# A recurrence and gated-MLP kernel: second products of tiles 5 to 7 in float16 parts, chunk ends copied by ScalarE, and GpSimd's work moved to VectorE in a new order

## The chip, the cores and the metric

The kernel runs on one core of a Trainium2 chip. The metric is device time in microseconds, the median of several executions. One further execution is profiled; its trace gives every duration below.

## The reference

Two computations follow each other. The first is a gated linear recurrence over 768 steps for 4 batches of 8 heads of 48 dimensions; the second is an MLP on the 3072 tokens that come out, with 384 inputs, 2048 hidden units and 384 outputs.

```python
f = 1.0 / (1.0 + np.exp(-f_logit))
for t in range(S):
    state = f[:, :, t, :, None] * state + einsum('bhd,bhe->bhde', k[:, :, t], v[:, :, t])
    y[:, :, t] = einsum('bhd,bhde->bhe', q[:, :, t], state)
x = y.transpose(0, 2, 1, 3).reshape(B * S, H * D)
h = x @ w_in
g = h * np.clip(h + 3.0, 0.0, 6.0) / 6.0
out = g @ w_out
```

## The kernel before

**Work and stages.** Time is cut into 6 chunks of 128 steps; a unit is one chunk of one batch, so there are 24 units, numbered 0 to 23 (unit i is chunk i // 4). Four units of one chunk make a group of 512 tokens for the MLP, so there are 6 groups. The 2048 hidden units are 16 tiles of 128; step `mm1.20` is the first product of tile 20 % 16 = 4 in group 20 // 16 = 1.

**A unit.** `gate` (ScalarE) takes the sigmoid of the gates. `back` (VectorE, line 428) is a scan from the right over a chunk: it gives the suffix products of the gates, in a buffer `suffix` of which there are three. `kmul` (line 441) multiplies k by them. Column 0 of the suffix buffer is then the product over the whole chunk, the chunk end. `turn` (step `rend`, lines 444 and 445) limits it from below into `ends`, and writes the reciprocal into `rend`. `fwd` (line 448) scans from the left, starting at `rend`, and overwrites the same suffix buffer; `qmul` (line 454) multiplies q by the result. `decay` multiplies the batch's state by `ends`. TensorE transposes k (`tk`, line 516), multiplies k and v (`kv`, 537), k and q (`att`, 497), q and the state (`qs`, 571), and, after `mask` (VectorE, line 504), the masked square and v (`av`, 587).

**The MLP.** Weights come as 64-bit floats and are turned by `z`, `cy`, `mid`, `dif`, `top`, `high` and `low` (or `lowi` and `lowo`, the halves of `low` for the first and the second product, line 320) into one 32-bit form (`wide`) and two float16 parts (`weight`). A first product of a tile takes nine float16 matmuls: three of the four pairs of parts times three blocks of the 384 inputs. In group 0, tiles 0 to 4 are computed in two halves of 256 tokens (`mm1a`, `mm1b`, line 828, with second products in float32, line 846). Tiles 5 to 7 have a whole first product (`mm1`, line 664), then `relu` and `g`, and a second product `mm2x` in float32 (line 720). From tile 8 on, `gh` (ScalarE, line 683) and `gl` (VectorE, line 693) split the activation into two float16 parts, and `mm2` (line 709) takes nine float16 matmuls:

```python
def mm2(g, f, ms=range(KT)):
    for i in range(3):
        a, b = P3[-i]
        for m in ms:
            nc.tensor.matmul(g["o"][m], wout[:, f, a, m * 128:(m + 1) * 128], g[f]["gg"][:, b], ...)

def mm2_whole(g, f):
    for m in range(KT):
        nc.tensor.matmul(g["o"][m], wide_out(f, m), g[f]["t"], ...)
```

Groups 2 to 5 compute first products by `p1` to `p8` (line 772), with sums of weight blocks.

**What sets the order.** The list `ORDER` names some 1,560 steps. Each engine, and the queue of SyncE that starts the loads, executes its share of the list strictly in that order. Step `warm.n` is a matmul on zeros of n blocks of 128 columns (line 1071), whose result nobody reads. `ON_POOL` lists the elementwise steps that run on GpSimd; all others of their kind run on VectorE.

Of the kernel before, what the change touches and what calls it, by code (L numbers as in the profile page):

```python
# [58 lines left out]
z.0 mid.0 loadq.2 gate.3 back.3 ld.1 carry0.1 warm.1 qs.1.0 dif.0 kmul.2 top.0 fwd.2 xl.0 carry1.1 loadq.3 av.1 hole.0
tk.2.4 rend.3 xh.1 xs.1 xl.1 z.1 qmul.2 warm.5 att.2.2 kmul.3 cy.1 mid.1 fwd.3 ktok.2 loadv.2 high.0 warm.4 kv.2.1  # L60
carry0.2 tk.3.4 ktok.3 mask.2 load.4 gate.4 qs.2.0 hole.1 av.2 xh.2 carry1.2 lowi.0 mm1a.0.4 relua.0 dif.1 qmul.3
top.1 high.1 ga.0 loadv.3 xs.2 att.3.2 mask.3 kv.3.1 ld.2 carry0.3 carry1.3 lowi.1 xl.2 loadq.4 warm.1 qs.3.2 av.3
xh.3 mm1a.1.4 cy.2 xs.3 xl.3 relua.1 z.2 back.4 kmul.4 rend.4 fwd.4 ga.1 decay.4 mm2a.0 qmul.4 load.5 gate.5 tk.4.1
mm2a.1 ktok.4 loadv.4 ld.3 cy.3 z.3 hole.2 mid.2 dif.2 top.2 att.4.2 kv.4.3 hole.3 mm1b.0.0 high.2 back.5 mid.3
relub.0 loadq.5 mm1b.1.1 relub.1 lowi.2 gb.0 dif.3 kmul.5 rend.5 gb.1 mm1a.2.4 mm1b.2.0 top.3 mm2b.0 mm2b.1 fwd.5
tk.5.1 relua.2 relub.2 gb.2 qmul.5 ld.4 z.4 cy.4 mid.4 mm2b.2 high.3 ktok.5 lowi.3 ga.2 mm1b.3.0 load.6 gate.6 loadq.6
dif.4 back.6 top.4 load.7 mm1a.3.4 ld.5 relub.3 mm2a.2 relua.3 ga.3 high.4 gb.3 cy.5 z.5 mask.4 mm2a.3 lowi.4 mm1a.4.1
relua.4 rend.6 ld.6 mm1b.4.4 relub.4 loadv.6 gate.7 loadq.7 mm2b.3 carry0.4 kmul.6 fwd.6 mid.5 ga.4 dif.5 z.6 qmul.6
top.5 cy.6 tk.6.1 ktok.6 mm2a.4 back.7 ld.7 decay.5 high.5 qs.4.2 decay.6 att.5.0 gb.4 av.4 kv.6.1 carry1.4 lowi.5
mm1.5.4 mask.5 mm2b.4 carry0.6 xh.4 z.7 xl.4 mid.6 dif.6 kmul.7 carry1.6 loadv.5 kv.5.3 ld.8 relu.5 g.5 mm2x.5 cy.7  # L70
top.6 high.6 cy.8 rend.7 tk.7.0 mid.7 dif.7 load.8 lowi.6 carry0.5 top.7 mm1.6.4 ktok.7 qs.5.2 fwd.7 qmul.7 high.7
loadv.7 relu.6 g.6 z.8 decay.7 att.6.0 ld.9 lowi.7 gate.8 av.5 cy.9 z.9 mask.6 mm1.7.4 relu.7 mid.8 dif.8 top.8 mid.9
carry1.5 dif.9 high.8 low.8 mm2x.6 mm1.8.0 g.7 loadq.8 ld.10 top.9 xh.5 cy.10 relu.8 high.9 back.8 rend.8 mm2x.7 ld.11
xl.5 g.8 att.7.2 z.10 cy.11 qs.6.0 kv.7.3 mid.10 load.10 loadv.8 av.6 dif.10 low.9 top.10 z.11 mid.11 gh.8 mm1.9.4
ld.12 ld.14 xh.6 xl.6 gl.8 mm2.8 dif.11 high.10 low.10 relu.9 g.9 cy.12 mm1.10.1 top.11 mask.7 kmul.8 carry0.7 gh.9
gl.9 hole.4 relu.10 high.11 mm2.9 carry1.7 g.10 low.11 z.12 mid.12 ld.13 dif.12 top.12 cy.13 gh.10 gl.10 tk.8.1 ktok.8
mm1.11.0 z.13 high.12 qs.7.2 mm2.10 av.7 loadq.9 ld.15 kv.8.3 decay.8 relu.11 mid.13 dif.13 low.12 loadv.9 mm1.12.1
g.11 gh.11 xh.7 top.13 carry0.8 high.13 xl.7 hole.7 gl.11 relu.12 z.14 z.15 low.13 fwd.8 qmul.8 mm2.11 g.12 gh.12
mm1.13.4 relu.13 g.13 cy.14 gh.13 gl.13 gl.12 mm2.12 cy.15 qs.8.2 mid.14 dif.14 att.8.0 mask.8 lowo.0 top.14 high.14
hole.6 hole.5 mm1.16.4 load.9 mid.15 mm1.17.1 relu.16 carry1.8 relu.17 dif.15 ws1.0 g.16 mm1.20.0 g.17 loadq.11 low.14  # L80
gate.10 xtop.0 gate.9 mm1.18.1 load.11 top.15 relu.18 loadq.10 back.9 high.15 gh.16 av.8 back.10 mm1.14.4 g.18 mm2.13
lowo.4 gh.17 relu.14 low.15 g.14 gh.14 mm1.15.1 mm1.19.4 lowo.6 gh.18 kmul.9 gl.18 rend.9 relu.15 g.15 lowo.3 gh.15
gl.14 gl.15 tk.9.1 lowo.5 lowo.1 mm2.14 fwd.9 mm2.15 gl.16 ktok.9 gl.17 outs.2 loadv.11 lowo.7 outv.1 outs.0 mm1.23.1
mm2.16 gate.11 lowo.2 ws2.0 relu.19 od.0 ws3.0 mm2.17 rend.10 xh.8 g.19 back.11 od.2 kmul.10 relu.20 decay.9 relu.23
kmul.11 hole.8 fwd.10 rend.11 od.1 load.13 qmul.10 xsum.0.2 g.20 g.23 mm1.21.4 relu.21 load.12 xleast.0 tk.10.3 ws4.0
qmul.9 decay.10 ktok.10 mm2.18 gh.19 g.21 mm1.25.3 gh.20 mm1.24.2 gh.21 loadv.10 gate.12 wtop.4 gl.19 relu.24 att.9.1
relu.25 kv.9.0 gl.20 fwd.11 g.25 carry0.9 loadv.12 g.24 wsh.0 load.14 qmul.11 mm1.22.4 gate.13 relu.22 back.12 gh.24
mm2.19 tk.11.3 gl.21 ws1.1 mask.9 gh.23 carry1.9 ktok.11 mm2.20 g.22 qs.9.0 att.11.3 gate.14 loadq.12 gh.25 gl.25 av.9
# [1150 lines left out]
```

## Time and profile before

| | us |
|---|---|
| median of 3 executions (lowest, highest) | 459.32 (459.2, 459.85) |
| the profiled execution: its time | 459.1 |
| the profiled execution: its span | 457.4 |
| TensorE busy in the span | 449.4 (98%) |
| VectorE busy | 359.3 (79%) |
| ScalarE busy | 231.2 (51%) |
| GpSimd busy | 19.0 (4%) |

The span runs from the first to the last instruction of the execution; 1.7 us of its time lie around it. Busy time is the union of an engine's records, and neighbouring records overlap a little, so the distance from one start to the next is a better price of an instruction in a full queue than its duration.

### The profile page before, as it was taken

To read this page: it belongs to the slowest core of one execution; us is meant where nothing else is said; L and a number is where in the kernel's file an instruction comes from. 1 tells how busy PE (TensorE), PEld (TensorE's weight loads), DVE (VectorE), ACT (ScalarE), POOL (GpSimd) and SP (SyncE) were. 2 spreads that over 40 slices of the span, in tenths; PEclk is the share of its full clock that TensorE was granted. 3 is DMA by queue.
4 is the path that set the end of the run, shared out by engine and by line. 5 is a ranking of instruction groups with operands and counts; after the bars stand their busy time and mean duration, and the time that the engine had idled before them with its cause. 6 is when DMAs were issued, how large, how long until landed. Compare 5 with 4: busy or idle time off the path is not lost.

```text
span 457.4 us, 12555 instructions
## 1 busy us (share of the span) xinstructions
PE 449.4 (98%) x5445; PEld 292.8 (64%) x5449; DVE 359.3 (79%) x643; ACT 231.2 (51%) x389; POOL 19.0 (4%) x31
## 2 busy tenths in 40 slices
...
GB/s 283 223 251 385 225 189 251 203 155 16 52 125 99 158 52 59 108 3 120 89 1 85 78 142 18 21 143 2 1 10 1 5 29 2 1 115 2 1 0 73
DMA packets 25531, 43.18 MB, mean 94 GB/s; under 512 B 2560, under 2 KB 17408, under 8 KB 25472
## 3 DMA queue, kind: packets, MB, share of 16 engines
...
## 4 chain that ended last, share of the span: by engine, by line
PE 94%; DVE 2%; DMA 1%; ACT 1%; issue 0%; SPq 0%; ACTq 0%
PE o L709 35%; PE pair L772 16%; PE single L772 9%; PE pair L664 7%; PE single L664 5%; PE o L846 3%; PE pair L497 3%; PE pair L587 3%; PE pair L571 3%; PE pair L537 2%; PE o L720 2%; PE pair L516 2%; PE o_half L862 1%; PE pair L862 1%; PE single L828 1%; PE pair L828 1%
## 5 line engine op out<-in xcount | busy, mean ns | idle before, releaser
L709 PE MATMUL o<-gg,weight 128*128 128x512 f16 x744 | 173.5, 379 | 0.1
L709 PEld LDWEIGHTS <-weight 128*128 128x128 f16 x744 | 71.7, 98 | 73.8
L772 PEld LDWEIGHTS <-weight 128*128 128x128 f16 x672 | 65.1, 98 | 13.3 <-issue 0.2
L772 PE MATMUL pair<-xmem,wide 128*128 128x256 f16 x384 | 51.2, 273 | 0.1
L683 ACT ACTIVATE gg<-raws 128x512 f16<-128x512 f32 x64 | 38.4, 624 | 23.9 <-DVE raws L806 8.1
L772 PE MATMUL single<-xmem,weight 128*128 128x256 f16 x384 | 49.8, 273 | 0.2 <-DVE raws L806 0.2
L801 ACT ACTIVATE raws<-pair,half 128x512 f32<-128x512 f32 x32 | 21.5, 684 | 42.7 <-PE pair L772 33.7
L772 PEld LDWEIGHTS <-wide 128*128 128x128 f16 x384 | 36.9, 98 | 8.7 <-DVE single L787 0.6
L801 ACT ACTIVATE raws<-single,half 128x512 f32<-128x512 f32 x32 | 22.0, 687 | 40.0 <-PE single L772 32.4
L664 PEld LDWEIGHTS <-weight 128*128 128x128 f16 x243 | 23.1, 98 | 26.8 <-issue 0.3
L772 PE MATMUL pair<-xmem,weight 128*128 128x256 f16 x288 | 36.5, 273 | 0.0
L806 DVE SCALAR_TENSOR_TENSOR raws<-raws,single 128x512 f32<-128x512 f32 x32 | 21.8, 682 | 18.4 <-ACT raws L801 18.4
L693 DVE TENSOR_TENSOR gg<-raws,gg 128x512 f16<-128x512 f32 x48 | 31.9, 682 | 5.0 <-ACT gg L683 5.0
L664 PE MATMUL pair<-xmem,weight 128*128 128x512 f16 x144 | 33.2, 379 | 0.0
L787 DVE TENSOR_TENSOR pair<-pair,raws 128x512 f32<-128x512 f32 x16 | 11.2, 697 | 25.5 <-PE pair L772 17.2
L806 DVE SCALAR_TENSOR_TENSOR raws<-raws,pair 128x512 f32<-128x512 f32 x32 | 21.5, 681 | 12.3 <-ACT raws L801 12.1
L448 DVE TENSOR_TENSOR_SCAN suffix<-gates,rend 112x516 f32<-112x516 f32 x24 | 29.7, 1236 | 0.1
L428 DVE TENSOR_TENSOR_SCAN suffix<-gates,unit 112x516 f32<-112x516 f32 x23 | 28.1, 1224 | 0.5 <-ACT gates L422 0.5
L664 PE MATMUL single<-xmem,weight 128*128 128x512 f16 x99 | 23.2, 380 | 0.1
L674 ACT ACTIVATE tg<-pair,half 128x512 f32<-128x512 f32 x16 | 10.9, 687 | 19.5 <-PE pair L664 16.3
L683 ACT ACTIVATE gg<-tg 128x512 f16<-128x512 f32 x24 | 14.4, 626 | 9.1 <-DVE tg L678 5.2
L504 DVE TENSOR_TENSOR a<-pair,causal 128x512 f32<-128x512 f32 x24 | 16.3, 682 | 1.2 <-PE pair L537 1.2
...
## 6 DMA issues: line engine op xcount, KB each, us to landing
...
```

Of the source, the lines that this page charges most:

```text
L428: nc.vector.tensor_tensor_scan(flat(sf)[:, ::-1], gt[:, 1:][:, ::-1], flat(unit)[:, ::-1], 0.0, op0=ALU.mult, op1=ALU.add,)
L448: nc.vector.tensor_tensor_scan(flat(sf), gt[:, :NP * (C + 1)], flat(rend), 0.0, op0=ALU.mult, op1=ALU.add,)
L497: nc.tensor.matmul(d["at"][HC * odd:HC * (odd + 1), e, 2 * n + c], t[rs, 1, n, c, odd], t[rs, 0, n, c, odd], start=not growing[at], stop=T ...
L504: nc.vector.tensor_tensor(d["a"].rearrange("r p e t -> r e p t"), d["at"], causal.unsqueeze(1).unsqueeze(1).broadcast_to([128, 2, NP, HC]) ...
L571: nc.tensor.matmul(d["y"][to:to + 64, odd, n, cs], before[rs, p], t[rs, 0, n, c, odd], start=alone and (odd, e) not in seen, stop=False, s ...
L664: nc.tensor.matmul(h, win[:, f, a, k * 128:(k + 1) * 128], g["xt"][:, k, :g["n"] // C, b], start=i == 0, stop=i == 3 * KT - 1,)
L683: nc.scalar.activation(d["gg"][:, 0], d["t"], AF.Copy)
L693: engine("gl", int(g["name"]) * NF + f).tensor_tensor(d["gg"][:, 1], d["t"], d["gg"][:, 0], op=ALU.subtract)
L709: nc.tensor.matmul(g["o"][m], wout[:, f, a, m * 128:(m + 1) * 128], g[f]["gg"][:, b], start=f == 0 and i == 0, stop=f == NF - 1 and i == 2 ...
L772: nc.tensor.matmul(to[:, n * 256:(n + 1) * 256], weights(q, n, a), g["wide"][:, :, block - 3, b], start=fresh and count == 1, stop=count = ...
L801: nc.scalar.activation(to, src, AF.Relu, bias=half, scale=RISE)
L806: nc.vector.scalar_tensor_tensor(to, to, TOP, src, op0=ALU.min, op1=ALU.mult)
```

## The change

- **Second products of tiles 5 to 7.** The three `mm2x` are gone. In their place stand `gh`, `gl` and `mm2` of these tiles.
- **Chunk ends.** A new ScalarE step `ends` copies column 0 of the suffix buffer into `ends`; the limit from below is dropped, and `rend` is the reciprocal taken from the suffix buffer directly. `fwd`, which overwrites that buffer, now has to wait for a ScalarE instruction.
- **GpSimd.** Fifteen steps leave `ON_POOL`, and `low.8` enters it.
- **The order.** The list is another one from its first lines on; `warm` has 44 blocks instead of 39, all before unit 3 is finished. At the end, `count` (line 985, the matmul that adds up the kernel's checks of its numbers) stands ahead of the matmul on zeros `seed.1` (line 809); before, it stood behind it.

```diff
 ON_POOL = """
-kmul.1 decay.4 kmul.6 lowi.5 kmul.7 decay.7 lowi.7 kmul.8 gl.9 decay.8 gl.11 qmul.8 gl.12 lowo.0 low.14
+low.8
 """.split()
 ORDER = """
-load.0 loadh.0 gate.0 gateh.0 back.0 backh.0 loadq.0 loadv.0 rend.0 kmul.0 load.1 fwd.0 gate.1 back.1 warm.16 tk.0.3
+load.0 loadh.0 gate.0 gateh.0 back.0 backh.0 loadq.0 loadv.0 ends.0 rend.0 kmul.0 load.1 warm.16 fwd.0 tk.0.4 ktok.0
...
+        def close():
+            nc.scalar.activation(ends[:, i], sf[:, :, 0], AF.Copy)
+
         def turn():
-            nc.vector.tensor_scalar_max(ends[:, i], sf[:, :, 0], END_LIMIT)
-            nc.vector.reciprocal(rend[:, :, 0], ends[:, i])
+            nc.vector.reciprocal(rend[:, :, 0], sf[:, :, 0])
...
-            "kmul": kmul, "rend": turn, "fwd": forward,
+            "kmul": kmul, "ends": close, "rend": turn, "fwd": forward,
```

Lines of the changed kernel behind this place are 4 higher than before (mm2 is line 713 there), and those between the list and this place 2 higher.

VectorE, the beginning of its queue. Before, from the scan of unit 0 (two halves) to the right-hand scan of unit 2 (`ends` and `rend` as above, `qkf` is k and q of a unit, `a` the masked square, and the suffix buffers 77, 79 and 81 belong to units 0, 1 and 2):

```order
L394 SCALAR_TENSOR_TENSOR suffix_77<-gates_76,unit 112x258 x2
L444 TENSOR_SCALAR ends<-suffix_77 112x4
L445 RECIPROCAL rend<-ends 112x4
L441 TENSOR_TENSOR qkf_137<-qkf_137,suffix_77 112x512
L448 SCALAR_TENSOR_TENSOR suffix_77<-gates_76,rend 112x516
L428 SCALAR_TENSOR_TENSOR suffix_79<-gates_78,unit 112x516
L454 TENSOR_TENSOR qkf_137<-qkf_137,suffix_77 112x512
L444 TENSOR_SCALAR ends<-suffix_79 112x4
L445 RECIPROCAL rend<-ends 112x4
L504 TENSOR_TENSOR a_216<-pair_70,causal 128x2x4x64
L448 SCALAR_TENSOR_TENSOR suffix_79<-gates_78,rend 112x516
```

The same queue of the changed kernel, to the same scan and one further:

```order
L396 SCALAR_TENSOR_TENSOR suffix_77<-gates_76,unit 112x258 x2
L449 RECIPROCAL rend<-suffix_77 112x4
L443 TENSOR_TENSOR qkf_137<-qkf_137,suffix_77 112x512
L452 SCALAR_TENSOR_TENSOR suffix_77<-gates_76,rend 112x516
L458 TENSOR_TENSOR qkf_137<-qkf_137,suffix_77 112x512
L430 SCALAR_TENSOR_TENSOR suffix_79<-gates_78,unit 112x516
L508 TENSOR_TENSOR a_204<-pair_70,causal 128x2x4x64
L443 TENSOR_TENSOR qkf_183<-qkf_183,suffix_79 112x512
L449 RECIPROCAL rend<-suffix_79 112x4
L430 SCALAR_TENSOR_TENSOR suffix_81<-gates_80,unit 112x516
L452 SCALAR_TENSOR_TENSOR suffix_79<-gates_78,rend 112x516
```

The q product of unit 0 now stands ahead of the scan of unit 1, the k product of unit 1 (`kmul.1`, row L443 on `suffix_79`) has come from GpSimd, and the limit (L444) is gone. Further on, the scans from the right of units 5 and 4 and `mid.2` stand ahead of `lowi.1`, the low part that the first product of tile 1 needs, and `ga.0` behind it; before, all four were the other way round.

TensorE, the second product of tile 5. Before, after the k-v products of unit 5 (L537), three float32 matmuls, and then the transposes of unit 7:

```order
L537 MATMUL pair_71<-v_912,ktok_714 48x48
L720 MATMUL o_0_572<-tg_5_931,wide 128x512
L720 MATMUL o_1_573<-tg_5_931,wide 128x512
L720 MATMUL o_2_574<-tg_5_931,wide 128x512
L516 MATMUL pair_70<-ident,qkf_792 128x112 x4
```

Now, where the rows of weight loads between them are left out:

```order
L713 MATMUL o_0_600<-gg_5_998,weight 128x512
...
L713 MATMUL o_1_601<-gg_5_998,weight 128x512
...
L713 MATMUL o_2_602<-gg_5_998,weight 128x512
```

These three rows stand three times, for the three pairs of parts, and read the float16 parts `gg_5` of the activation instead of the float32 tile `tg_5`.

ScalarE, the copy of the chunk end of unit 4 in the changed kernel (`th_0` is the `relu` of tile 0, behind its first product; L624 and L612 write MLP inputs out of PSUM):

```order
L612 ACTIVATE xmem<-pair_70 112x4x128
L624 ACTIVATE xmem<-pair_71 112x4x128
L841 ACTIVATE th_0_567<-single,half 128x256
L624 ACTIVATE xmem<-pair_70 112x4x128
L446 ACTIVATE ends<-suffix_79 112x4
L290 ACTIVATE wide<-raws 128x2x384
L841 ACTIVATE th_1_587<-pair_71,half 128x256
```

The copy stands behind instructions that read products of TensorE, so VectorE's scan of unit 4, which overwrites `suffix_79`, now depends on them too; before, no row of ScalarE read a suffix buffer.

## Rows read from the trace of the kernel before

**Rows 1.** The page: busy time, share of the span, instructions of each engine.

```profile
span 457.4 us, 12555 instructions
PE 449.4 (98%) x5445; PEld 292.8 (64%) x5449; DVE 359.3 (79%) x643; ACT 231.2 (51%) x389; POOL 19.0 (4%) x31
```

**Rows 2.** Windows: length, busy us (instructions) per engine, TensorE clock, DMA share, GB/s.

```profile
0.00:30.00 30.00, 26.17 (x572) 16.92 (x573) 25.23 (x45) 16.89 (x33) 4.17 (x17) 1.00 0.78 280
45.00:120.00 75.00, 75.00 (x881) 42.05 (x879) 67.32 (x116) 50.55 (x75) 14.30 (x13) 1.00 0.46 163
120.00:240.00 120.00, 119.90 (x1639) 75.22 (x1640) 112.50 (x204) 59.90 (x104) 0.00 (x0) 1.00 0.26 82
240.00:450.00 210.00, 209.71 (x2170) 143.00 (x2171) 137.06 (x241) 91.13 (x158) 0.00 (x0) 1.00 0.12 36
```

**Rows 3.** TensorE's own waits: us in total, times, longest.

```profile
PE pair L497 <- DVE qkf L454: 0.9, 2, 0.7
PE pair L537 <- ACT ktok L523: 0.6, 1, 0.6
```

**Rows 4.** The chain that ended last: start, length, what.

```profile
67.98 2.58 PE o L720 x6
...
87.89 2.05 PE o L709 x9
...
116.68 3.89 PE o L709 x18
```

**Rows 5.** Timeline of VectorE near the start: start, length, what, idle before.

```profile
8.05 1.23 DVE L428 TENSOR_TENSOR_SCAN suffix<-gates,unit 112x516 f32<-112x516 f32 x1 [0.51 <-ACT gates L422]
...
9.79 1.16 DVE L444 TENSOR_SCALAR ends<-suffix 112x4 f32<-112x4 f32 x1
...
15.32 0.16 DVE L444 TENSOR_SCALAR ends<-suffix 112x4 f32<-112x4 f32 x1
15.52 0.18 DVE L445 RECIPROCAL rend<-ends 112x4 f32<-112x4 f32 x1
15.61 0.35 DVE L301 TENSOR_SCALAR raws<-top 128x768 int16<-128x768 int16 x1
```

**Rows 6.** Timeline of GpSimd: its first product of the order.

```profile
9.50 1.42 POOL L441 TENSOR_TENSOR qkf<-qkf,suffix 112x512 f32<-112x512 f32 x1 [5.76 <-DMA qkf<-qk]
```

**Rows 7.** Timeline of VectorE around the low part of tile 1.

```profile
27.24 0.42 DVE L841 SCALAR_TENSOR_TENSOR th<-th,single 128x256 f32<-128x256 f32 x1 [0.97 <-ACT th L837]
...
28.26 0.55 DVE L320 TENSOR_TENSOR weight<-wide,weight 128x384 f16<-128x384 f32 x1
28.73 1.23 DVE L428 TENSOR_TENSOR_SCAN suffix<-gates,unit 112x516 f32<-112x516 f32 x1
```

**Rows 8.** Timeline of TensorE: the first product of tile 1.

```profile
29.89 1.16 PE L828 MATMUL single<-xmem,weight 128*128 128x256 f16 x9
```

**Rows 9.** VectorE by line and form: busy us, mean ns, idle before.

```profile
L428 DVE TENSOR_TENSOR_SCAN suffix<-gates,unit 112x516 f32<-112x516 f32 x23 | 28.1, 1224 | 0.5 <-ACT gates L422 0.5
...
L454 DVE TENSOR_TENSOR qkf<-qkf,suffix 112x512 f32<-112x512 f32 x23 | 15.5, 680 | 0.1
...
L693 DVE TENSOR_TENSOR gg<-tg,gg 128x512 f16<-128x512 f32 x21 | 13.8, 677 | 0.9 <-ACT gg L683 0.7
...
L320 DVE TENSOR_TENSOR weight<-wide,weight 128x384 f16<-128x384 f32 x13 | 7.1, 552 | 0.2 <-ACT weight L317 0.2
...
L457 DVE TENSOR_TENSOR decayed<-state,ends 112x192 f32<-112x192 f32 x17 | 5.9, 347 | 0.0
```

**Rows 10.** ScalarE by line and form: its shortest activation.

```profile
L253 ACT ACTIVATE table<-half 128x1 f32<-128x1 f32 x1 | 0.2, 204 | 0.9 <-POOL half L251 0.9
```

**Rows 11.** Timeline of the end, all engines.

```profile
452.96 0.17 DVE L981 TENSOR_SCALAR sound<-sums 128x31 f32<-128x31 f32 x1
...
453.13 0.38 PE L809 MATMUL pair<-blank 128*128 128x512 f16 x1
...
453.44 0.23 PE L985 MATMUL pair<-sound,ones 128*1 128x36 f32 x2
```

More of the change, by code (lines that the diff above doesn't have):

```diff
@@ L59 @@
[L59 to L88, printed above, removed]
@@ new lines @@
+att.5.0 ktok.6 lowo.5 high.6 top.7 mask.5 mm1.5.4 ld.8 carry1.5 mask.4 fwd.6 loadv.7 high.7 kv.6.2 qs.5.1 z.9 relu.5
+mid.9 ld.10 cy.8 g.5 av.4 av.5 lowi.7 dif.9 decay.6 z.8 xh.4 top.9 qmul.6 mm1.7.4 mid.8 gh.5 mm2a.4 carry0.6 gate.7
+cy.10 ld.11 lowi.6 carry1.6 z.10 att.6.0 qs.6.2 dif.8 relu.7 load.9 load.8 mid.10 top.8 gl.5 xh.5 high.9 dif.10 high.8
+mm2b.4 mask.6 xl.5 g.7 mm2.5 av.6 ld.12 top.10 back.7 low.9 cy.11 cy.12 low.8 ends.7 mm1.6.1 mm1.8.4 loadq.8 xl.4 xh.6
+mm1.9.0 relu.6 loadv.8 xl.6 g.6 high.10 kmul.7 low.10 rend.7 z.11 tk.7.2 gh.6 lowo.6 gl.6 fwd.7 ktok.7 gh.7 mid.11
@@ new lines @@
+qmul.7 loadq.9 mm1.10.1 lowo.7 mm2.6 ld.13 dif.11 gl.7 z.13 hole.5 hole.4 att.7.3 top.11 decay.7 kv.7.2 mm2.7 relu.8
+relu.9 relu.10 z.12 high.11 mask.7 carry0.7 g.8 gh.8 loadv.9 cy.13 low.11 qs.7.3 g.9 mid.12 gl.8 g.10 mm1.11.4 load.10
+av.7 dif.12 loadv.10 gh.9 carry1.7 mm2.8 gate.10 gl.9 gate.8 gh.10 ld.14 xh.7 top.12 relu.11 mid.13 gate.9 mm2.9 xl.7
+g.11 loadq.11 hole.6 high.12 low.12 z.14 back.8 dif.13 cy.14 ld.15 mm1.12.2 hole.7 relu.12 mid.14 top.13 dif.14 cy.15
+g.12 top.14 mm1.18.3 high.13 relu.18 gl.10 low.13 g.18 kmul.8 gh.11 high.14 mm1.16.4 mm1.17.0 z.15 gl.11 gh.12 ends.8
@@ new lines @@
+mid.15 mm1.13.2 low.14 relu.13 relu.17 gl.12 g.13 g.17 mm1.14.3 gh.13 dif.15 mm1.20.1 rend.8 top.15 relu.14 tk.8.2
+back.10 ws1.0 mm2.10 g.14 high.15 gh.18 ktok.8 low.15 mm2.11 back.9 ends.10 ws2.0 mm1.15.2 mm1.25.0 gl.18 xtop.0
+kmul.9 fwd.8 load.11 relu.16 relu.15 lowo.0 g.15 gl.13 gh.17 mm2.12 gh.14 mm2.13 ws3.0 qmul.8 gl.14 mm2.14 ends.9
+loadq.10 att.8.2 gh.15 lowo.4 ws4.0 rend.9 ws1.1 kv.8.3 gl.15 gate.11 decay.8 g.16 mm1.23.4 mask.8 ws2.1 gh.16 kmul.10
+carry0.8 gl.17 mm2.15 gl.16 carry1.8 fwd.9 rend.10 outs.0 outs.2 lowo.2 od.2 outv.1 qmul.9 back.11 seed.0.2 mm1.19.3
```

143 lines of the change are left out of this document (80 added, 63 removed).

## The prediction

> **What bounds the kernel now.** I read the page first: TensorE is busy for 449.4 of 457.4 us, VectorE for 359.3, ScalarE for 231.2, GpSimd for 19.0 [rows 1]. An average says little here, so I read windows next. From 45 to 450 us TensorE is busy all but 0.4 us of 405, at full clock throughout; only the first 30 us hold real idle time, 3.8 us [rows 2]. Its waits say the same: the two costliest besides the launch are 0.9 us for a q product of VectorE and 0.6 us for a copy of ScalarE, both at the start [rows 3]. So the time is TensorE's work, plus what the start loses, plus the end. The second thing to see is how near VectorE comes: from 45 to 120 us it is idle for 75.0 − 67.3 = 7.7 us, from 120 to 240 us for 7.5, and only behind that does it have room, 73 us [rows 2]. An edit that shortens TensorE's queue is worth its full length as long as VectorE keeps ahead.
>
> **The second products.** In the chain one float32 `mm2x` takes 2.58 us in six passes; nine float16 matmuls in a row take 2.05 alone and 3.89 for eighteen, so 1.94 each in a full queue [rows 4]. Three tiles give 3 × (2.58 − 1.94) = 1.9 us less on the engine that binds. For it ScalarE gets three `gh` (it is idle half of the time, [rows 1]), and VectorE three `gl`. These lie beside other products unless VectorE is late.
>
> **VectorE's bill.** Records in a full queue overlap by some 0.08 us: the low part at 28.26 us lasts 0.55, and the next begins 0.47 later [rows 7]. Taking 0.08 off each mean [rows 9], a product of 512 columns costs 0.60, a half low part 0.47, a decay 0.27, a scan 1.14. Behind 45 us VectorE takes from GpSimd `kmul` of three units, `qmul.8` and three `gl` (7 × 0.60), two decays (0.54) and three half low parts (1.41); `low.14` and `low.8` change places. With the three new `gl` (1.8) that is 8.0 us. Against it stand the limits: `ends` starts at 15.32 and the work behind the pair at 15.61, while the reciprocal alone costs 0.09 [rows 5], so each unit saves 0.20 us, 4.8 in all, some six units of them (1.2) by 120 us. ScalarE pays 24 short activations of about 0.2 us [rows 10], 5 us on an engine with 226 idle.
>
> **A row that changes the bill.** One `ends` took 1.16 us where the next took 0.16 [rows 5]. It began at 9.79, and GpSimd was multiplying from 9.50 to 10.92 [rows 6]; the reciprocal could not follow before that was over. So `kmul.1` on GpSimd cost VectorE 1.0 us where VectorE itself needs 0.60. The Trainium skill, page "SBUF — State Buffer", section "Who interferes with whom", states that the two engines share a port pair as an exclusive lock, and that the one that starts second blocks until the other is done. The trace agrees to 0.03 us here. By the rule any other two-input VectorE instruction behind a GpSimd one would be blocked as well, and the 14 later steps would come back with a discount of up to their own 15 us on GpSimd; I take none, since only one such delay has a row here.
>
> **The start.** Here a path has to be added up. In the kernel before, VectorE is done with the low part of tile 1 at 28.73 us [rows 7], and the first product of tile 1 starts at 29.89 [rows 8]. To that point the changed queue adds `kmul.1` (0.60), two scans (2.28) and `mid.2` (0.27, the interval of L301 taken as a decay's); it drops `ga.0` (the 0.42 us record at 27.24, less 0.08: 0.34), three limits (0.60; that of unit 0 only covered a load) and the blocked 1.0. Two waits go too: 0.51 us for the sigmoid of unit 1, which `qmul.0` now fills [rows 5], and 0.97 for the `relu` in front of `ga.0` [rows 7]. The sum is 28.73 + 3.15 − 0.34 − 0.60 − 1.0 − 0.51 − 0.97 = 28.5. TensorE then has behind it what it had at 29.89, so this product starts up to 1.4 us earlier, with two scans already done. Five more `warm` blocks, 0.2 us each at the 2.58 / 12 us that 128 float32 columns take [rows 4], stand where TensorE waits for VectorE, and cost nothing as long as it does; if it did not, 1.1 us. The bounds of the start are thus 0 and −1.4. Behind it each low part and each `ga`, `gb` comes only a few tenths ahead of the product that needs it, and a short wait of VectorE passes straight on. I take −1.0.
>
> **The stretch from 45 to 120 us.** VectorE had 67.3 us of work. It gets 8.0, saves 1.2, and enters with two scans (2.3) done ahead: 67.3 + 8.0 − 1.2 − 2.3 = 71.8 of 75.0 us. It fits, but adding steps up in their order, the low part of tile 12 used to be ready 7 us ahead of its product and is now ready about 0.4 ahead. I take 0.5 us of new TensorE waits; the bounds are 0 and the slower rival's sum below.
>
> **The wait that is added.** The scan `fwd` must wait for ScalarE's copy. Behind it on VectorE stand the q product, and with it `att` and `qs`, and low parts. For unit 4 the copy stands behind the `relu` of tile 0 and a PSUM read, and the same addition puts the copy near 29 us, the scan near 34. In the later chunks the copy stands behind other `relu`s, but VectorE has room there [rows 2]. I take nothing; the upper bound is the second rival.
>
> **The end.** `count` began at 453.44 us, behind a matmul on zeros from 453.13, and its input was ready at 452.96 + 0.17 [rows 11]. Put ahead, it gains up to 0.2 us; the last output's transfer may bind instead. I take 0.1.
>
> **Sum.** 459.1 (the profiled execution) − 1.9 − 1.0 + 0.5 − 0.1 = 456.6. The median of the runs shown is 0.2 above the profiled one, so the forecast is 456.8 us, 0.55% less. This kernel's measurement tells about 0.2% (0.9 us) from no change.
>
> **Rivals.**
> - *VectorE becomes the bound (slower).* If VectorE goes on losing its 7.7 us of waits between 45 and 120 us, it needs 71.8 + 7.7 = 79.5 us for a stretch of 75, and TensorE waits 4.5: 459.3 − 1.9 − 1.0 − 0.1 + 4.5 = 460.8. It decides against the change from 3.0 us of new waits on. For it speaks the thin lead. Against it: those waits were for ScalarE and TensorE, because VectorE was ahead, and they shrink when it is not. The Trainium skill, "Perfetto Trace Analysis", section "Optimizing Scalar/DVE Operations", advises moving work away from a saturated VectorE, to ScalarE or even GpSimd, and adds that between VectorE and GpSimd it might not help as they share a port. This change goes the other way for GpSimd. No run here shows yet which half holds.
> - *The start gives nothing.* The scans wait for `ends` behind ScalarE's copies, or the transfers, in another order, come late. 459.3 − 1.9 + 0.5 − 0.1 = 457.8.
> - *All leads hold.* No new waits and the whole start: 459.3 − 1.9 − 1.4 − 0.2 = 455.8.
> - *No change.* The 1.9 us come back as waits at `mm2` of tiles 5 to 7: `gh` and `gl` put 0.6 + 0.6 us between `g` and the second product, and these tiles lie where VectorE is fullest. With a start that gains nothing this ends at 459.2.
>
> **How the numbers follow.** Chances: the forecast 0.52, all leads hold 0.12, the start gives nothing 0.14, no change 0.10, slower 0.12. The range goes from 455.3, which is 0.5 below the case in which all leads hold (an end or a GpSimd out of the way that gives more), to 459.0, which leaves out the slower case and part of no change. Faster by more than 0.2% means below 458.4: the first three cases, 0.78. Within 0.2%: 0.10. Slower: 0.12.
>
> **What would show it.** TensorE's line for float32 512-column products is gone, and the line of `mm2` has 27 instructions more. The first product of tile 1 starts between 28.5 and 29.5 us. No `ends` record lasts over 0.3 us. VectorE is busier between 45 and 120 us, about 95%, and TensorE's idle time there stays below 1 us. I am wrong if TensorE's waits for VectorE lines (low parts, `gl`, masks) come to 2 us or more between 30 and 130 us, or if scans of line 452 wait for ScalarE at the start.

## The result, and the profile after

The changed kernel takes 461.40 us (median of 13 runs, 458.44 to 464.24), the kernel before on the same chips 458.88 (13 runs, 458.56 to 459.85): a ratio of 1.0059 with a 95% interval of 1.0033 to 1.0084. It is slower where 0.55% faster was forecast. The new kernel's runs scatter over 5.8 us, the old one's over 1.3, and the time goes with the mean clock that TensorE was granted: seven runs at 0.995 to 0.999 took 458.44 to 461.40 us, six at 0.988 to 0.993 took 462.53 to 464.24. The profiled run is the slowest of them (464.24, at 0.989), so its trace shows a loss of 5.1 us against the profiled run of before, where the median run loses 2.5.

The page gives TensorE's share [rows 1], and the packets and MB of the queue that brings instructions:

```profile
span 462.5 us, 12604 instructions
PE 453.5 (98%) x5474; PEld 297.3 (64%) x5474; DVE 361.7 (78%) x636; ACT 233.8 (51%) x416; POOL 4.4 (1%) x17
...
q8 instruction: 43, 0.70, 0.6%
```

Windows of the same stretches as before [rows 2], and of 10 to 20 and 20 to 30 us:

```profile
0.00:30.00 30.00, 26.70 (x474) 18.78 (x474) 20.54 (x35) 14.53 (x31) 2.75 (x16) 0.83 0.70 250
45.00:120.00 75.00, 73.57 (x833) 42.21 (x832) 72.29 (x127) 51.84 (x84) 1.65 (x1) 1.00 0.50 174
120.00:240.00 120.00, 120.00 (x1738) 74.74 (x1739) 110.25 (x189) 57.07 (x106) 0.00 (x0) 1.00 0.29 89
240.00:450.00 210.00, 209.45 (x2207) 144.26 (x2198) 140.23 (x242) 94.89 (x169) 0.00 (x0) 1.00 0.11 32
```

```profile
10.00:20.00 10.00, 7.83 (x155) 6.77 (x154) 9.38 (x15) 5.00 (x11) 0.00 (x0) 0.81 0.93 348
20.00:30.00 10.00, 10.00 (x227) 7.35 (x225) 4.86 (x7) 5.44 (x11) 0.00 (x0) 0.68 0.39 143
```

TensorE looks as busy in the first 30 us as before, but it ran 474 instructions there in place of 572: the eighth column, its clock, is 0.83 in place of 1.00. VectorE did 25.23 us of work there before and now 20.54: it was not overfull, it stood idle for 9.5 us. TensorE's waits say what was (line numbers are a few higher than before, and differ a little from kernel to kernel):

```profile
PE pair L501 <- issue: 1.8, 1, 1.8
...
PE pair L668 <- DMA xmem<-xmem: 0.9, 1, 0.9
PE pair L520 <- issue: 0.6, 1, 0.6
```

"issue" means that nothing the profile records ended the wait: no engine, no transfer. TensorE's timeline at that place:

```profile
11.79 1.27 PE L1075 MATMUL idle<-blank 128*128 128x128 f32 x6
...
14.29 0.46 PE L501 MATMUL pair<-qkf 48*64 48x64 f32 x16 [0.17 <-DVE qkf L458]
16.56 0.71 PE L501 MATMUL pair<-qkf 48*64 48x64 f32 x16 [1.81 <-issue]
17.20 2.93 PE L1075 MATMUL idle<-blank 128*128 128x128 f32 x12
...
33.85 1.15 PE L832 MATMUL single<-xmem,weight 128*128 128x256 f16 x9
...
35.29 1.16 PE L832 MATMUL pair<-xmem,weight 128*128 128x256 f16 x9
```

One step, `att.1`, is torn in two: 16 of its 32 matmuls run, then TensorE stands for 1.81 us. Both halves read the same `qkf`, which was there for the first. Behind the gap six blocks of 128 columns of zeros (a step leaves two records, x12) take 2.93 us, 0.49 each; at 11.79 five (x6, as one step holds three blocks) took 1.27, 0.25 each. The granted clock is at half (1.2 GHz) from 16.1 to 26.3 us. The first product of tile 1 starts at 35.29, in place of 29.89 [rows 8]. The delay passes to the other engines, as VectorE's timeline shows:

```profile
11.02 0.17 DVE L449 RECIPROCAL rend<-suffix 112x4 f32<-112x4 f32 x1
...
21.58 1.23 DVE L452 TENSOR_TENSOR_SCAN suffix<-gates,rend 112x516 f32<-112x516 f32 x1 [1.66 <-ACT ends L446]
...
27.18 0.36 DVE L303 TENSOR_SCALAR raws<-top 128x768 int16<-128x768 int16 x1 [2.37 <-ACT top L299]
```

From the first product of tile 1 to the end it is 462.5 − 35.29 = 427.2 us, before 457.4 − 29.89 = 427.5. So all of this run's loss lies ahead of 36 us.

### The profile page after: what moved, and what is told of

Same layout as the page of the kernel before. It is cut to its first block, busy times and chain, and to the rows that moved or that the text cites. A ratio compares the mean times of both kernels' runs of the same rounds, so it can differ in the third digit from the quotient of the medians.

```text
span 462.5 us, 12604 instructions
## 1 busy us (share of the span) xinstructions
PE 453.5 (98%) x5474; PEld 297.3 (64%) x5474; DVE 361.7 (78%) x636; ACT 233.8 (51%) x416; POOL 4.4 (1%) x17
## 4 chain that ended last, share of the span: by engine, by line
PE 88%; DVE 5%; ACT 3%; DMA 2%; issue 1%; ACTq 0%
PE o L713 34%; PE pair L776 16%; PE single L776 9%; PE pair L668 5%; PE single L668 4%; PE pair L501 3%; PE idle L1075 3%; PE o L850 2%; PE pair L591 2%; PE pair L575 2%; PE pair L541 2%; PE pair L832 2%; DMA raws<-w 2%; PE pair L520 1%; PE o_half L866 1%; PE pair L866 1%
## 5 line engine op out<-in xcount | busy, mean ns | idle before, releaser
L713 PE MATMUL o<-gg,weight 128*128 128x512 f16 x771 | 179.1, 379 | 0.0
L713 PEld LDWEIGHTS <-weight 128*128 128x128 f16 x771 | 74.5, 98 | 76.1
L776 PEld LDWEIGHTS <-weight 128*128 128x128 f16 x672 | 64.7, 98 | 12.1 <-issue 0.5
L668 PEld LDWEIGHTS <-weight 128*128 128x128 f16 x243 | 22.9, 98 | 28.1 <-DMA xmem<-xmem 1.4
L668 PE MATMUL pair<-xmem,weight 128*128 128x512 f16 x144 | 32.7, 379 | 0.9 <-DMA xmem<-xmem 0.9
L668 PE MATMUL single<-xmem,weight 128*128 128x512 f16 x99 | 23.2, 380 | 0.0
L687 ACT ACTIVATE gg<-tg 128x512 f16<-128x512 f32 x27 | 16.3, 623 | 12.5 <-PE o L713 8.9
L501 PE MATMUL pair<-qkf 48*64 48x64 f32 x768 | 16.6, 225 | 2.0 <-issue 1.8
```

The costliest lines, as they stand in the source:

```text
L501: nc.tensor.matmul(d["at"][HC * odd:HC * (odd + 1), e, 2 * n + c], t[rs, 1, n, c, odd], t[rs, 0, n, c, odd], start=not growing[at], stop=T ...
L668: nc.tensor.matmul(h, win[:, f, a, k * 128:(k + 1) * 128], g["xt"][:, k, :g["n"] // C, b], start=i == 0, stop=i == 3 * KT - 1,)
L687: nc.scalar.activation(d["gg"][:, 0], d["t"], AF.Copy)
L776: nc.tensor.matmul(to[:, n * 256:(n + 1) * 256], weights(q, n, a), g["wide"][:, :, block - 3, b], start=fresh and count == 1, stop=count = ...
```

## What stops TensorE: the experiments

**Counting records.** Every matmul leaves a record on PE and one for its weights on PEld; the trace also holds TensorE's few waiting instructions (58 in all, 8 of them ahead of the gap), which the page does not count as busy. Counted together in order of start, the gap in `att.1` lies behind record 449. The page has 43 packets on the instruction queue for 5474 + 5474 + 58 records, 256 a packet. The theory: TensorE's instructions come in packets of 256, the next packet is fetched while the current one runs, and when TensorE runs 256 records faster than a packet arrives, it stands still, and then loses its clock. The rival: VectorE's and ScalarE's fuller start is the cause, and the gap only shows it. The kernels in the table are those of the experiments below. From the traces, in us (records 193 and 449 open and close one packet; the packet named is the one needed behind it):

| kernel | record 193 starts | packet fetched | record 449 starts | record 450 starts |
|---|---|---|---|---|
| before | 10.44 | 13.79 to 14.75 | 15.97 | 16.21 |
| changed | 9.67 | 14.37 to 15.32 | 14.53 | 16.56 |
| later_loads | 10.33 | 13.47 to 14.42 | 15.19 | 15.78 |
| act_loads | 9.72 | 13.94 to 14.89 | 14.58 | 16.36 |
| warms_first | 9.52 | 14.57 to 15.52 | 15.28 | 16.90 |
| warms8_hole | 9.62 | 12.69 to 13.64 | 15.74 | 15.75 |
| before_small_blocks | 9.17 | 13.17 to 14.13 | 13.70 | 15.49 |

In the kernels that stop, record 450 starts 1.24 to 1.47 us after its packet has landed. In the kernel before it is 1.46, and 0.24 us lie between the starts of records 449 and 450, where records a few hundredths of a us apart stand on either side: the kernel before had nothing to spare here. It took 5.53 us from record 193 to 449, the changed kernel 4.86. That time alone does not decide: warms_first took 5.76 us and stopped, since the fetch of its packet began 5.05 us behind record 193; in the kernel before it began 3.35 us behind.

**More records, nothing else (before_small_blocks).** The six first steps of zeros of the kernel before, issued as blocks of 128 columns (x16 stands for sixteen times):

```diff
-warm.16 tk.0.3 ktok.0 warm.4 kv.0.1
+warm.1 x16 tk.0.3 ktok.0 warm.1 x4 kv.0.1
...
-warm.3 att.1.0 xs.0 loadv.1 back.2 mask.1 rend.2 cy.0 load.3 warm.3 kv.1.3
+warm.1 x3 att.1.0 xs.0 loadv.1 back.2 mask.1 rend.2 cy.0 load.3 warm.1 x3 kv.1.3
```

> The kernel before, with the first six steps of zeros (warm.16, warm.4, twice warm.1, twice warm.3) issued as single blocks of 128 columns: the same columns of zeros, the same order, 76 TensorE records more before kv.1. Instruction supply: TensorE stands at its 449th record, about 1 us earlier than before, at 14.5 to 15 us, before the packet is usable, waits 0.5 to 2 us with no engine and no transfer as the end of the wait, in some runs with clock lost behind it, and the median is 459.5 to 463. VectorE's queue as the whole cause: nothing changes, 458.4 to 459.2, no such wait.

Measured: 463.03 us (460.87 to 465.01, 6 runs; before 459.09), ratio 1.0084 [1.006, 1.0108]. TensorE's timeline, and a window behind its second gap:

```profile
13.55 0.42 PE L612 MATMUL pair<-xmem,less 112*112 112x256 f16 x2
15.49 0.83 PE L1071 MATMUL idle<-blank 128*128 128x128 f32 x6 [1.52 <-issue]
...
29.06 0.57 PE L587 MATMUL pair<-a,v 64*64 64x64 f32 x23
32.01 0.47 PE L587 MATMUL pair<-a,v 64*48 64x64 f32 x9 [2.39 <-issue]
```

```profile
32.00:37.00 5.00, 4.99 (x26) 3.89 (x26) 1.30 (x4) 3.38 (x6) 0.00 (x0) 0.50 0.03 7
```

The stops lie behind records 449 and 1217, three packets apart, and the clock is at half from 31.4 to 38.2 us, from the second stop on. Old order, old data, the same columns: 76 records more cost 3.9 us. Here the theory stands, and the rival falls as the whole cause: VectorE's queue was untouched.

**The zeros moved or lengthened in the new order (warms_first, warms8_hole, warms16_hole).** The six blocks that stood behind `att.1` go ahead of `kv.1` in two longer steps; then eight blocks there, with `ld.15` behind `hole.7` (a `hole` is a transfer of SyncE that fills the rest of a unit's MLP input, `xmem`); then eight more behind `kv.3`:

```diff
-z.0 kv.1.0 att.1.1 warm.1 carry0.1
+z.0 warm.4 warm.2 kv.1.0 att.1.1 carry0.1
...
-rend.3 warm.1 warm.1 warm.1 qmul.2
+rend.3 qmul.2
```

> The changed kernel with the six blocks of zeros that stood between att.1 and tk.2 (six warm.1) issued ahead of kv.1 instead, as warm.4 and warm.2: the same columns, in 8 TensorE records fewer. TensorE then comes to its 448th record about 1.3 to 1.5 us later. Theory A (TensorE runs out of instructions at record 448, because the next packet of them lands at about 15.2 us, and the clock falls behind that gap): the wait in the middle of att.1 shrinks from 1.8 us to 0.7 or less, the granted clock of 10 to 30 us is above 0.9, the first product of tile 0 starts before 31.5 us and that of tile 1 before 33, and the median is 457.5 to 459.5. Theory B (the kernel is slow because VectorE and ScalarE have too much to do at the start and behind it, and the gap only shows it): the idle time goes to waits for VectorE, the first product of tile 1 stays at 34 to 35 us, and the median is 461 to 462.

```diff
-z.0 warm.4 warm.2 kv.1.0
+z.0 warm.4 warm.4 kv.1.0
...
-cy.14 ld.15 mm1.12.2 hole.7
+cy.14 mm1.12.2 hole.7 ld.15
```

> As the kernel with the zeros ahead of kv.1, with two blocks of zeros more there (warm.4 twice) and with ld.15 behind hole.7 in SyncE's queue. Theory A: no wait for instructions of over 0.3 us in att.1, no clock below 1.00 behind 10 us, no wait for the hole of mm1.18 at 94 us (it was 0.9 us): 456.5 to 458.5, faster than both kernels if the stretch behind 30 us holds as summed. Theory B: 460.5 to 462, the two blocks more cost 0.4.

```diff
-gate.4 kv.3.2 top.0
+gate.4 kv.3.2 warm.4 warm.4 top.0
```

> As the kernel with eight blocks of zeros ahead of kv.1 and ld.15 behind hole.7, with eight blocks more (warm.4 twice) behind kv.3, so that TensorE comes to its 961st record 1.7 us later, at about 26.9 us, when the packet of instructions is there. Instruction supply as the whole loss: no wait of over 0.4 us without an engine or a transfer as its end, no stretch of half clock behind 10 us, the first product of tile 1 at 31 to 31.5 us in place of 32.8, 458.3 to 459.3 us. VectorE as the loss: TensorE waits for VectorE lines instead, first product of tile 1 at 32.5 or later, 460.5 to 462.

Measured: 461.06 (460.63 to 462.63), 461.86 (460.71 to 463.91) and 461.73 (459.93 to 463.41), beside 458.7 to 458.8 for before. In warms_first the stop shrank only to 1.40 us, as the packet came no earlier (at 14.57), and one of 0.98 came behind record 705. In warms8_hole the stop at 449 is gone and `tk.2` starts at 16.54 in place of 19.92, but it stands behind record 961, 512 records on:

```profile
25.09 0.34 PE L574 MATMUL pair<-qkf,middle 48*64 48x64 f32 x6 [0.33 <-ACT middle L553]
26.96 0.44 PE L574 MATMUL pair<-qkf,middle 48*64 48x64 f32 x10 [1.53 <-issue]
```

In the profile of warms16_hole only a stop of 0.72 (record 705) is left, and the clock holds:

```profile
15.00:30.00 15.00, 13.64 (x397) 10.22 (x400) 13.73 (x21) 11.29 (x22) 0.00 (x0) 1.00 0.83 283
...
31.82 1.15 PE L831 MATMUL pair<-xmem,weight 128*128 128x256 f16 x9
```

So the place of the stop moves by whole packets, as the theory wants, and in this profile no half clock is left. But the medians do not fall. With nearly all of the stop gone, tile 1 still starts at 31.8, two microseconds behind the kernel before. Three of the six runs of warms16_hole have a mean clock of 0.993 to 0.996, so they lost clock somewhere that the profiled run did not; yet the three at 0.999 to 1.000 also took 459.9 to 462.9. So "instruction supply is the whole loss" falls too.

**The loads (later_loads, act_loads, before_early_loads).** Does the packet come late because weight and input transfers stand ahead of it? In the changed kernel `loadq.3`, `ld.1` and `loadv.2` went behind `load.4`, or were started by ScalarE behind `gate.3`; in the kernel before `ld.2` and `loadv.2` went behind `loadv.1`:

```diff
-loadq.2 warm.1 loadq.3 rend.1 warm.3 ld.1 gate.2
+loadq.2 warm.1 rend.1 warm.3 gate.2
...
-qmul.2 load.4 load.5
+qmul.2 load.4 loadq.3 ld.1 loadv.2 load.5
```

> The changed kernel, with three loads (k and q of unit 3, weights of tile 1, v of unit 2) put behind the load of the gates of unit 4 in SyncE's queue, so that they start at about 13.5 us instead of 9 to 10. Nothing else is moved. Theory 1 (TensorE ran out of instructions at 14.75 us because their fetch stood behind the loads, and the 1.8 us without work took the clock to half for 10 us): the fetch starts by 12 us, TensorE has no wait of over 0.6 us near 15 us, the granted clock stays 1.0, the first product of tile 1 starts near 29 us instead of 35.3, and the median falls by 4 to 6 us to 456 to 457.5. Theory 2 (VectorE is too full without GpSimd, TensorE waits for it and loses its clock so): the wait and the clock stay, 460 to 463.

```diff
-nc.sync.dma_start(out=raw[:, 1:4 * WN + 1], ...)
+(nc.scalar if f"ld.{f}" in ON_ACT else nc.sync).dma_start(out=raw[:, 1:4 * WN + 1], ...)
```

> The changed kernel, with the loads of k and q of unit 3, of the weights of tile 1 and of v of unit 2 started by ScalarE behind the sigmoid of unit 3, at about 13 us, instead of by SyncE at 9 to 10. Fewer bytes are then under way when TensorE asks for its next instructions (near 11 us), and no load waits for the gates of unit 4 as it did where they were put behind these in SyncE's queue. Theory 1 (late instructions, then half clock): the fetch packet starts before 13 us, no wait of TensorE over 0.3 us without a releaser near 15 us, clock 1.0, the first product of tile 1 near 29.5 us, median 456.5 to 458. Rival (the start of the new order is no faster even when nothing is late, and the 1.9 us of the second products go to waits behind 45 us): clock 1.0 but 458.5 to 459.5. Theory 2 (VectorE too full): 460 to 463.

```diff
-loadv.1 back.2
+loadv.1 ld.2 loadv.2 back.2
```

> The kernel before, with two loads more at the beginning (weights of tile 2 and v of unit 2 put ahead of the gates of unit 3), 1 MB, some 2.4 us at 400 GB/s. Theory 1: the first fetch of TensorE's instructions starts about 2.4 us later than at 13.9 us, near 16.3, the instructions come at about 18 us, and TensorE, which needs them at 17.2, stands still for 0.5 to 1.5 us without a wait for another engine; the clock may fall, time 459.5 to 463. Theory 2: VectorE's work is the same, so 459 and no wait.

Measured: 460.86 (459.23 to 465.49), 460.04 (457.56 to 463.71) and 459.75 (459.18 to 461.97), ratios 1.0048 [1.0023, 1.0072], 1.003 [1.0005, 1.0054] and 1.002 [1.0008, 1.0032]. later_loads has the smaller stop (0.37): its record 449 starts 0.66 us later than the changed kernel's, and its packet lands 0.90 us earlier. It buys a new wait with it, and neither it nor act_loads comes to the 456 to 458 us that a packet on time should have given:

```profile
22.28 0.91 PE L540 MATMUL pair<-v,ktok 64*64 64x48 f32 x48 [1.02 <-DMA v<-v]
```

Counted from record 193, the packet's fetch starts 3.1 us after in later_loads, 4.2 in act_loads, 4.7 in the changed kernel. So far loads out of the way go with an earlier packet. But in before_early_loads, with 1 MB more ahead of it, it starts 3.3 us after, as in the kernel before (3.35), and no stop of over 0.4 us follows, where 0.5 to 1.5 was expected; and warms_first and warms8_hole, whose early loads are the same, differ by 2.0 us (5.1 and 3.1). That the packet queues behind the load bytes is thus not shown, with one profile each; why its fetch starts 2.7 to 5.1 us after record 193 stays open.

**The price of the clock (before_few_warms).** The kernel before without its nine later steps of zeros:

```diff
-ktok.0 warm.4 kv.0.1
+ktok.0 kv.0.1
...
-qmul.1 warm.3 att.1.0
+qmul.1 att.1.0
```

> The kernel before, without its nine later warm steps (23 blocks; the first, of 16, stays). TensorE then does nothing in places where it did work on zeros. Price of a lost clock by itself: if the clock falls for 3.4 us or more in the first 30 us, the time rises by 1.5 to 5 us, 460.5 to 464; if it holds, the time stays at 459 or falls by a few tenths, since TensorE waits for VectorE there anyway.

Measured: 462.67 (461.39 to 463.54), ratio 1.0085 [1.0071, 1.01]. In its window the clock is 0.66:

```profile
15.00:30.00 15.00, 11.73 (x292) 9.27 (x285) 11.62 (x20) 8.82 (x17) 0.00 (x0) 0.66 0.71 252
```

Here it is mostly waits for other engines that leave TensorE idle, 0.4 to 1.0 us at several places and 2.0 us for a q product of VectorE until 20.72 us. The clock is at half from 18.9, the beginning of that last wait, to 29.1 us. So lost clock is not peculiar to instruction stops, and 3.6 us is the price of the waits and the clock together.

## The parts of the change, one by one

**In the order of before (split_only, ends_only, pool_only, old_order_all).** One edit alone each, then all three: `mm2x` of tiles 5 to 7 to `gh`, `gl`, `mm2` with `lowo.5` to `lowo.7` behind `lowi`; an `ends` step on ScalarE ahead of each `rend`; all of GpSimd's steps but `low.8` on VectorE.

```diff
-g.5 mm2x.5
+g.5 gh.5 gl.5 mm2.5
...
-rend.5
+ends.5 rend.5
...
-kmul.1 decay.4 kmul.6 lowi.5 kmul.7 decay.7 lowi.7 kmul.8 gl.9 decay.8 gl.11 qmul.8 gl.12 lowo.0 low.14
+low.8
```

> The kernel before, with the second products of tiles 5 to 7 in float16 parts alone: gh and gl behind g, mm2 in the place of mm2x, and the low parts of these tiles' second weights moved up behind those of the first. GpSimd keeps its steps, the order is that of before. The prediction's first term: 1.9 us less on TensorE if VectorE, which gets 1.8 us of gl and 1.4 us of low parts earlier, keeps ahead: 457.0. Its rival: the time comes back as waits at mm2 of tiles 5 to 7, 458.5 to 459.5.

> The kernel before, in its order and with its GpSimd steps, with one edit alone: the chunk ends are copied by ScalarE directly ahead of each reciprocal, without limit. If the added wait costs nothing, as the sum has it: 458.5 to 459.2, since VectorE saves 0.2 us a unit where it leads. If reciprocal or scan wait behind ScalarE's queue: 460 to 463, with waits of TensorE for VectorE lines whose own wait is for ends.

> The kernel before in its order, with one edit alone: all GpSimd steps but low.8 on VectorE. If VectorE's room of 7.7 us between 45 and 120 us covers them, as the sum has it: 458 to 460 (kmul.1 alone gives up to 1.0 us at the start). If the order was made for GpSimd's part: 461 to 466, with waits of TensorE for low parts and products of VectorE between 45 and 120 us.

> The kernel before in its own order, with all three edits (second products split, chunk ends copied by ScalarE right ahead of each reciprocal, GpSimd left with low.8 alone). Theory 1: the loads and TensorE's place at the first fetch are as before, no half clock, so 456.5 to 458.5 with some waits for VectorE. Theory 2: VectorE has 9 us more to do up to 120 us in an order that was not made for it, so TensorE waits and the clock falls, 460 to 464.

Measured: 464.45 (1.0122 [1.0107, 1.0136]), 463.66 (1.01 [1.0085, 1.0114]), 463.80 (1.0103 [1.0088, 1.0117]) and 472.88 (1.03 [1.0285, 1.0314]). Each edit alone costs 5 us, all together 14. TensorE's longest waits, of split_only (two rows), ends_only and pool_only:

```profile
PE single L663 <- DVE tg L677: 2.1, 1, 2.1
PE pair L496 <- DVE xmem L621: 1.7, 1, 1.7
```

```profile
PE o L849 <- DVE th L844: 1.8, 1, 1.8
```

```profile
PE o L709 <- DVE gg L693: 1.8, 1, 1.8
```

All three make TensorE wait for VectorE in the old order, and with the waits come stretches of half clock (0.89 from 60 to 75 us in split_only, and from 15 to 45 in ends_only). Of the four, only pool_only came out in an expected range; split_only, ends_only and old_order_all were slower than either expectation. The new order is what takes 11 of these 14 us away.

**Parts of the changed kernel undone (pool_back, float32_second, old_start).** GpSimd's fifteen steps back; the second products of tiles 5 to 7 in float32 again; the order of before up to `mm1a.1`, then the new one.

```diff
-gh.5
...
-gl.5
...
-mm2.5
+mm2x.5 lowo.5
```

```diff
-low.8
+kmul.1 decay.4 kmul.6 lowi.5 kmul.7 decay.7 lowi.7 kmul.8 gl.9 decay.8 gl.11 qmul.8 gl.12 lowo.0 low.14
```

> The changed kernel in its own order, with the fifteen steps back on GpSimd and low.8 back on VectorE. Theory 1: the start keeps its late instructions and half clock, so 459 to 463, within 1.5 us of the changed kernel. Theory 2: VectorE is relieved of 8 us, TensorE's waits between 45 and 120 us go, and the time falls to 457 to 459.

> The changed kernel with the second products of tiles 5 to 7 in float32 again (mm2x in the places of mm2, no gh and gl for them, lowo.5 to lowo.7 behind them), all else as changed. If the split is worth 1.9 us in the new order, as the sum has it: 462.8 to 463.8, at equal clock of the start. If the split is worth nothing because VectorE's part of it comes back as waits: 461 to 462.

> The beginning of the order of before, up to the first product of tile 1 (GpSimd's k product of unit 1 and all warm blocks with it, chunk ends by ScalarE ahead of each reciprocal), and behind it the changed kernel's order. Theory 1: TensorE reaches its first fetch as before, the clock holds; VectorE comes out of the start with two scans less done, 2.3 us, and waits of 1 to 3 us for it appear between 35 and 60 us: 457 to 460. Theory 2: the waits for VectorE and half clock are there as in the changed kernel, 460 to 464.

Measured: 462.51 (460.49 to 466.24, 1.0102 [1.0071, 1.0134]), 465.41 (461.88 to 466.98, 1.0138 [1.011, 1.0167]) and 463.90 (463.33 to 464.63, 1.0106 [1.0091, 1.0121]). pool_back shows a like stop (1.25 us), and the interval of its ratio overlaps the changed kernel's: no part of GpSimd in the loss can be seen here. It does show more of what the prediction had one row of. Seven VectorE instructions that start beside a GpSimd step last 0.3 to 1.0 us longer than the median of their line and shape, 4.0 us together, and each ends about its own usual length behind the GpSimd step's end, as this one of usually 0.35 us:

```profile
90.98 1.35 DVE L303 TENSOR_SCALAR raws<-top 128x768 int16<-128x768 int16 x1
```

```profile
90.75 1.36 POOL L443 TENSOR_TENSOR qkf<-qkf,suffix 112x512 f32<-112x512 f32 x1 [5.41 <-DVE suffix L430]
```

In the kernel before there are only two such instructions, 1.3 us together.

float32_second stops for 2.7 us behind record 961 and has 6.8 us of half clock behind that, so its median, slower than either expectation, mixes two things. From its first product of tile 1 on, at full clock, it takes 462.8 − 35.41 = 427.4 us; later_loads, which like it has hardly a wait for a hole transfer, takes 457.5 − 31.74 = 425.8. By this one pair of profiles the split is worth 1.6 us in the new order. In old_start TensorE waits 3.8 us at a transposition for ScalarE to read a product of a half tile (`th`). ScalarE's own queue makes it late: the read stands behind six other instructions there, which fill it from 31.39 us on with a wait of only 0.37 us for VectorE among them.

```profile
PE idle L1074 <- issue: 2.7, 1, 2.7
```

```profile
PE pair L519 <- ACT th L840: 3.8, 1, 3.8
```

```profile
31.39 0.62 ACT L423 ACTIVATE gates<-gates 112x512 f32<-112x512 f32 x1
...
34.43 0.21 ACT L445 ACTIVATE ends<-suffix 112x4 f32<-112x4 f32 x1 [0.37 <-DVE suffix L429]
34.54 0.89 ACT L289 ACTIVATE wide<-raws 128x768 int32<-128x768 uint32 x1
35.34 0.45 ACT L840 ACTIVATE th<-single,half 128x256 f32<-128x256 f32 x1
```

**Real work in the gap (tile0_early, tile0_early2).** From warms8_hole: `high.0`, `lowi.0`, `mm1a.0`, `relua.0` and `hole.0` early, `loadq.5` behind `hole.1`, so that TensorE multiplies tile 0 while the packet comes; in the second, `ld.2` behind `hole.1` as well.

```diff
-carry1.3 warm.4 mask.2 warm.1 hole.0 carry0.3 dif.1 carry1.2 high.0 qs.2.3
+carry1.3 high.0 warm.4 mask.2 lowi.0 carry0.3 dif.1 carry1.2 mm1a.0.4 qs.2.3
```

> As the kernel with eight blocks of zeros ahead of kv.1 and ld.15 behind hole.7, with real work ahead of record 961: high.0 behind carry1.3, lowi.0 behind mask.2, mm1a.0 ahead of qs.2, relua.0 ahead of xh.2, hole.0 behind ld.2, loadq.5 behind hole.1, and two blocks of zeros (warm.1) fewer. Instruction supply as the whole loss: mm1a.0 at 25.5 to 26.5 us, the first product of tile 1 at 29.5 to 30.5 us, clock 1.00 behind 10 us, 457 to 458.3 us, faster than the kernel before. VectorE as the loss: mm1a.0 waits for lowi.0 until 27 us or later, tile 1 at 32 or later, 460 to 462.

```diff
-kmul.3 ld.2 hole.0
+kmul.3 hole.0
...
-cy.1 hole.1 loadq.5
+cy.1 hole.1 ld.2 loadq.5
```

> As the kernel with the early product of tile 0, with ld.2 behind hole.1 in SyncE's queue, so that the hole transfers do not share the queues with 768 KB of weights. If the wait of mm1a.0 for its holes (1.24 us) was the start's last brake: mm1a.0 at 25.5 us, first product of tile 1 at 30.3 to 30.8 us, best run 457 to 457.8. If VectorE's own queue sets tile 1 (low part of tile 1 done at 30.1 us there): mm1a.0 earlier, tile 1 at 30.8 to 31.3, best run at 458.

Measured: 461.09 (458.10 to 463.72, 12 runs; 1.0046 [1.0023, 1.0068]) and 460.88 (460.20 to 464.28; 1.0053 [1.003, 1.0076]). In the profile of tile0_early no stop is over 0.4 us and the clock is 1.00 behind 10 us; tile 0 is multiplied as early as in the kernel before (25.93 against 25.54), and yet:

```profile
29.66 0.56 DVE L321 TENSOR_TENSOR weight<-wide,weight 128x384 f16<-128x384 f32 x1 [0.29 <-ACT weight L318]
30.14 0.55 DVE L309 TENSOR_TENSOR top<-top,raws 128x768 int16<-128x768 int16 x1
```

```profile
25.93 1.14 PE L831 MATMUL single<-xmem,weight 128*128 128x256 f16 x9 [1.24 <-DMA xmem<-xmem]
...
31.24 1.16 PE L831 MATMUL pair<-xmem,weight 128*128 128x256 f16 x9
```

The low part of tile 1 is done at 30.14, not at 28.5. VectorE's longest wait on the way there is for a sigmoid of ScalarE:

```profile
9.28 1.23 DVE L429 TENSOR_TENSOR_SCAN suffix<-gates,unit 112x516 f32<-112x516 f32 x1 [1.02 <-ACT gates L423]
```

In tile0_early2 tile 0 comes earlier still, at 24.40, but tile 1 only at 31.32, and its best run, 460.2, is slower than either expectation: ScalarE waits 2.06 us for the weights that were put back, the high part of tile 1 stands behind that in its queue, so VectorE waits 1.22 us for it, and TensorE waits 1.9 us for copies of ScalarE:

```profile
PE pair L615 <- ACT xmem L611: 1.9, 2, 1.1
```

No version beats the kernel before in the median; single runs do (457.56 in act_loads, 458.10 here, against 458.31 as the best of before).

## Why the prediction was wrong, step by step

**The second products (−1.9): right, as far as shown.** The line of float32 512-column products is gone, L713 has 27 instructions more (771), and one pair of profiles gives −1.6.

**VectorE's bill: right.** 72.29 us of work between 45 and 120 us, where 71.8 was summed, and no wait of TensorE for a VectorE line stands there. The blocked limit is gone with its line, and no reciprocal (L449) is over 0.18 us. The Trainium skill, page "SBUF — State Buffer", section "Who interferes with whom", on the shared lock, agrees with the two lengths of the limit (1.16 us beside GpSimd, 0.16 without [rows 5]) and with the seven longer instructions of pool_back. The discount that the prediction did not take was hardly there to take: two delays, 1.3 us, of which 0.3 lie behind 30 us.

**The start (−1.0, bounds 0 and −1.4): the step that failed.** It came out as +5.4 us in the profiled run (29.89 to 35.29). The prediction added up VectorE's queue alone and said of TensorE that it "then has behind it what it had" and that five more blocks of zeros, where TensorE waits, "cost nothing as long as it does". Two things were missing. First, TensorE's own supply: denser records at the start outran the packets (a stop of 1.81 us), and 10.2 us of half clock came with the stop. Second, VectorE's waits: two old ones were struck out and no new ones put in, though the copies of ScalarE, the sigmoids and the loads of the new order had to be waited for. Where TensorE does not stop (tile0_early), the low part is done at 30.14, 1.6 us behind the sum. VectorE's waits up to there are 1.7 us: 1.0 for the sigmoid of unit 1 (the very wait of 0.51 us that the sum had struck out), 0.4 for a q transfer (0.3 of it in the kernel before, too), 0.3 for the high part of ScalarE. So 1.4 us of waits are new to the sum. Even with a full supply of instructions the start gained nothing: tile 1 starts at 31.24 there, 1.35 us later than before, and the run took 459.78. The two best runs of tile0_early, 458.1 and 458.3, come near the rival "The start gives nothing", 457.8, but have no profile.

**45 to 120 us (+0.5): 1.4 us, from elsewhere.** TensorE is idle for 75.0 − 73.57 us: 0.9 for the hole transfer of a first product (L668) and 0.6 at 77.7 us, which the matmul's row puts down to issue and the row of the weight load ahead of it to ScalarE (at no packet's end by the count; unexplained), none for low parts. The prediction wanted less than 1 us here. **The wait on ScalarE's copy (0):** 1.66 us in the profiled run, one of the prediction's own signs of being wrong. It came behind TensorE's stop; in the profile of tile0_early, where TensorE does not stop, no scan at the start waits for it, so it looks like a result of the stop and not a cause. **The end (−0.1): −0.3.** The count now starts at once, at 458.55:

```profile
458.55 0.23 PE L989 MATMUL pair<-sound,ones 128*1 128x36 f32 x2
```

It takes 3.95 us from there to the end, as before [rows 11]; the matmul on zeros, 0.31 us, is out of its way.

**The sum by what was measured,** for the profiled run: 459.1 + 5.4 (start) − 0.3 (all behind tile 1: −1.6 to −1.9, +1.4, −0.3 and small waits) = 464.2, the time it took. The median run (461.40, at 0.996) has no profile. The profiled runs of other kernels at a mean of 0.996 (act_loads, warms8_hole, pool_back) each have one stretch of 3.4 us at half clock, so an estimate for it is half of that, 1.7 of the 2.5 us that it loses. Of the rivals none names the mechanism; "VectorE becomes the bound", at 460.8, is near in time by luck and wrong in cause. What stays open: why runs at nearly full mean clock still differ by up to 4 us (tile0_early: 458.3 and 462.6 at 0.999), since only one run of each kernel has a profile.
